# Attention and feed-forward kernel: seven buffers for the outputs of block products, sums by halves, and another order of the last pair's products

## Chip, cores and metric

One core of a Trainium2 chip. The time is device microseconds from the first to the last instruction as the host's timing of the execution sees it; the profile's own span is some 1.8 us shorter (214.0 against 215.77 for the same execution).

## The reference

```
scores = (q @ k^T) / 8, ALiBi bias, keep j if j < 8 or 0 <= i - j < 96   # batch 4, 8 heads, 768 rows, 64
x   = softmax(scores) @ v, heads side by side                            # 3072 x 512
h   = x @ w_in                                                           # 512 -> 2048
g   = s * relu(h)^2 + b
out = g @ w_out                                                          # 2048 -> 512, float32
```

## The kernel before

The rows are worked in 12 granules of 256. For each granule: scores on TensorE (PE), exponentials on ScalarE (ACT), mask on VectorE (DVE), product with v, normalization (DVE), then the first feed-forward matrix in "quarters" (`unit_p1`: 16 matmuls, two ReLUs, one square). The second matrix is applied to two granules (even `e` and odd `o`) together by a scheme of seven block products instead of eight. It needs sums of blocks of the left operand (`g_sum`, DVE), and each product is evicted into partial results or an output block that is stored.

```python
def unit_p1(j, q):
    ...                                   # 2 x (8 matmuls, ReLU on ACT)
    if j % 2:
        outs.append(lambda: nc.vector.tensor_tensor(gs, gs, gs, ALU.mult))
    else:
        nc.scalar.activation(gs, gs, ACT.Square)
...
def store(pr, row, col, ps, add):
    o = work.tile([P, GB, CH], F32, name="o_q", tag="o_sb", bufs=3)
    scaled(o[:].rearrange("p a c -> p (a c)"), ps, add)   # DVE: ps * s + add
    put(pr, row, col, o[:])                               # store on SP's queue
...
def step(s, c0, c1, c2, pool=None, pre=()):
    ...
    posts = scores(s + 1)      # PE; exponentials and masks of the next step
    run(exps); run(pre); run(masks)
    run(c0); stage_A(2 * s); flush()          # flush: evictions and squares put off
    run(c1); stage_A(2 * s + 1, pool); flush()
    run(c2) ...
    if not last and SHIFT < j + 1 < NJ:
        load_voff(j + 1, eng=nc.scalar)       # SBUF to SBUF loads, issued on ACT's queue
    flush()
...
# the last pair
run([u1(e, 2), u1(e, 3), pe(pr, 1), flush])
run([u1(o, 0), flush, g_sum(pr, 3, 0), u1(o, 1), flush, g_sum(pr, 3, 1)])
run([u1(o, 2), flush, g_sum(pr, 1, 0), g_sum(pr, 2, 0), pe(pr, 7), flush])
run([u1(o, 3), flush, g_sum(pr, 1, 1), g_sum(pr, 2, 1), pe(pr, 2), flush])
run([pe(pr, 5), flush, g_sum(pr, 4), pe(pr, 6), flush, join(pr, 1), join(pr, 2), join(pr, 0)])
run([pe(pr, 4), flush])
for tb in range(GB):                          # product 3 in halves of 128 rows
    ...
```

`pe(pr, n)` is product n of pair pr: two blocks of 128 x 256, eight matmuls each. A row of 32 matmuls in a timeline is two products.

## Time and profile before

| | before |
|---|---|
| time, first three executions | 215.04, 215.28, 216.84 us |
| span of the profiled execution | 214.0 us |
| busy: PE, DVE, ACT | 202.2, 156.6, 132.9 us |

PE is busy 95% of the span. In a timeline row the columns are start, length, engine, line, operation, output and inputs, shapes, count, and in brackets the idle time before it and what ended it. I measure PE from start to start. The best milestones are the score matmuls (`ps_s`), once a step: what lies between two of them is one step.

### The profile page before, as it was taken

Reading aid. Unit: us, or ns where it says so; the run is one execution under the profiler, and the core shown is the slowest. Engines: PE = TensorE matmul, PEld = TensorE weight load, DVE = VectorE, ACT = ScalarE, POOL = GpSimd, SP = SyncE. Lnnn points to the kernel's source line nnn. Section 1 sums busy time; section 2 is a strip of 40 time slices with the busy share of each in tenths; the row PEclk is TensorE's granted clock in tenths of the full one; section 3 lists DMA queues with packets and bytes.
Section 4 is the critical chain, followed back from the end, with each engine's and each line's share of the span. In section 5 each row is a group of like instructions: output and inputs, shape, how many; then the busy total and the mean of one; then the engine's idle time right before and its main releaser. Section 6 shows DMA issues by size and latency. Waiting matters only on the chain.

```text
span 214.0 us, 5315 instructions
## 1 busy us (share of the span) xinstructions
PE 202.2 (95%) x2181; PEld 159.8 (75%) x2189; DVE 156.6 (73%) x329; ACT 132.9 (62%) x203; POOL 68.9 (32%) x90
## 2 busy tenths in 40 slices
PE   6799999999998999999999999799999999999991
PEld 2578885557866585778788888688888889888880
DVE  3787579995989666877798874498683796726693
ACT  5765669486965558687664966554967763486300
POOL 8883335898645104507308264000000000000000
PEclk9999999999999999999999999999999999999998
DMA  6999999999999997999999979973232300330014
GB/s 171 197 178 204 207 206 174 153 152 129 117 145 132 158 158 149 142 273 208 174 150 172 141 108 192 192 106 73 51 130 72 98 5 0 98 101 0 0 52 147
DMA packets 109636, 28.43 MB, mean 133 GB/s; under 512 B 97804, under 2 KB 108108, under 8 KB 109612
## 3 DMA queue, kind: packets, MB, share of 16 engines
q0 software_dynamic: 72864, 12.85, 81.5%
q1 hardware_dynamic: 35056, 13.64, 35.9%
q10 hardware_dynamic: 1692, 1.61, 3.2%
q8 instruction: 17, 0.28, 0.6%
q14 instruction: 7, 0.06, 0.1%
HBM read 27.26 MB, written 6.29 MB: 157 GB/s over the span
## 4 chain that ended last, share of the span: by engine, by line
PE 64%; DVE 13%; DMA 8%; SPq 4%; ACT 4%; issue 3%; POOL 1%; ACTq 1%; POOLq 0%; DVEq 0%
PE ps L626 30%; PE ps L825 14%; PE ps L674 10%; DMA out_dram<-o_q 4%; PE ps_av L502 4%; DMA nat<-in_q_dram 3%; DVE gsum L789 3%; SPq L367 2%; PE ps_s L448 2%; DVE xn L473 2%; DVE pt L464 2%; DVE gT L800 2%; ACT pt L457 2%; SPq L606 2%; ACT gT L636 1%
## 5 line engine op out<-in xcount | busy, mean ns | idle before, releaser
L626 PE MATMUL ps<-xT,w_in_bf 128*128 128x256 bf16 x768 | 90.4, 273 | 1.2 <-DVE o_q L834 1.2
L636 ACT ACTIVATE gT<-ps 128x512 bf16<-128x512 f32 x96 | 56.1, 598 | 45.7 <-PE ps L626 45.3
L626 PEld LDWEIGHTS <-w_in_bf 128*128 128x128 bf16 x768 | 72.8, 98 | 10.2 <-issue 1.3
L457 ACT ACTIVATE pt<-ps_s 128x1024 bf16<-128x1024 f32 (+1 forms) x44 | 39.2, 944 | 6.3 <-PE ps_s L448 4.0
L674 PE MATMUL ps<-w_out_bf,gT 128*128 128x512 bf16 x120 | 28.7, 380 | 0.5 <-issue 0.2
L464 DVE TENSOR_TENSOR pt<-pt,tmpl 128x1024 bf16<-128x1024 bf16 (+1 forms) x40 | 24.9, 647 | 5.6 <-ACT pt L457 5.3
L825 PEld LDWEIGHTS <-gsum 128*128 128x128 bf16 x256 | 24.2, 98 | 4.6 <-DVE gsum L789 1.6
L105 POOL DMA_DIRECT2D nat<-in_k_dram x22 | 19.7, 895 | 8.2 <-DMA w_in_bf<-in_moe_w_in_dram 4.2
L106 POOL DMA_DIRECT2D vb<-in_v_dram x22 | 19.9, 906 | 7.0 <-DMA nat<-in_k_dram 2.6
L105 POOL DMA_DIRECT2D nat<-in_q_dram x22 | 19.9, 906 | 6.5 <-DMA w_out_bf<-in_moe_w_out_dram 3.4
L473 DVE TENSOR_TENSOR xn<-ps_av,rc 128x256 bf16<-128x256 f32 x48 | 20.4, 425 | 1.6
L674 PEld LDWEIGHTS <-gT 128*128 128x128 bf16 x128 | 11.7, 98 | 13.0
L825 PEld LDWEIGHTS <-gT 128*128 128x128 bf16 x192 | 18.6, 98 | 2.4
L502 PEld LDWEIGHTS <-pt 128*128 128x128 bf16 x320 | 14.1, 97 | 5.6 <-DVE xn L473 3.1
L802 ACT ACTIVATE gT<-gT 128x1024 bf16<-128x1024 bf16 x16 | 16.9, 1057 | 0.5
L639 DVE TENSOR_TENSOR gT<-gT 128x512 bf16<-128x512 bf16 x32 | 13.3, 422 | 5.2 <-ACT gT L636 4.7
L502 PE MATMUL ps_av<-vb,pt 128*128 128x65 bf16 x208 | 15.4, 194 | 1.4 <-DVE xn L473 1.2
L800 DVE TENSOR_TENSOR gT<-gT 128x1024 bf16<-128x1024 bf16 x16 | 11.0, 686 | 7.4 <-ACT gT L636 7.4
L825 PE MATMUL ps<-wsub,gsum 128*128 128x256 bf16 x128 | 14.9, 273 | 0.8 <-DVE gsum L789 0.8
L111 POOL COPY gate<-xT 1x1 bf16<-1x1 bf16 x6 | 2.6, 437 | 38.0 <-DMA xT<-xn 35.5
L825 PE MATMUL ps<-w_out_bf,gT 128*128 128x256 bf16 x128 | 14.8, 273 | 0.0
L472 DVE RECIPROCAL rc<-ps_av 128x4 f32<-128x4 f32 x48 | 8.5, 178 | 8.5 <-PE ps_av L502 6.6
(106 smaller groups left out, 215.5 us busy)
## 6 DMA issues: line engine op xcount, KB each, us to landing
out_dram<-o_q SPq DMA_DIRECT2D x15, 256.0 KB, 2.2
nat<-in_k_dram POOLq DMA_DIRECT2D x22, 128.0 KB, 7.4
nat<-in_q_dram POOLq DMA_DIRECT2D x22, 128.0 KB, 7.3
vb<-in_v_dram POOLq DMA_DIRECT2D x22, 128.0 KB, 8.1
w_in_bf<-in_moe_w_in_dram POOLq DMA_DIRECT2D x4, 512.0 KB, 11.4
w_out_bf<-in_moe_w_out_dram POOLq DMA_DIRECT2D x4, 512.0 KB, 17.9
out_dram<-o_sb SPq DMA_DIRECT2D x4, 256.0 KB, 5.1
out_dram<-o_early SPq DMA_DIRECT2D x4, 256.0 KB, 6.5
```

The source lines that it names most:

```text
L105: nc.gpsimd.dma_start(t[:, n, i, :, :], rows_of(srcs[n], b, sb))
L106: nc.gpsimd.dma_start(vbuf[b % 2][:, sb, :, 0:D], rows_of(v, b, sb))
L457: nc.scalar.activation(pt[:, :, 0:ncol], ps[:, :, 0:ncol], ACT.Exp, scale=QSCALE)
L464: nc.vector.tensor_tensor(pv, pv, m.rearrange("p h a c -> p h (a c)"), ALU.mult)
L473: nc.vector.tensor_tensor(dst, av[:, :, :, 0:D], rc[:].to_broadcast((P, 2, 2, D)), ALU.mult)
L502: nc.tensor.matmul(av[:, i, hi, 0 : D + 1], lhsT=pt[:, hi, c * P : (c + 1) * P], rhs=vv, start=(n == 0), stop=(n == len(terms) - 1),)
L626: nc.tensor.matmul(ps[:, i, :], lhsT=w_in_bf[:, kc, fc * P : (fc + 1) * P], rhs=xT[j][:, kc, :], start=(kc == 0), stop=(kc == KC - 1),)
L636: nc.scalar.activation(gs, ps[:], ACT.Relu)
L674: nc.tensor.matmul(po[:], lhsT=g_of(j)[:, fc, tb * P : (tb + 1) * P], rhs=w_out_bf[:, fc, :], start=(fc == 0), stop=(fc == FC - 1),)
L800: outs.append(lambda: nc.vector.tensor_tensor(gs, gs, gs, ALU.mult))
L802: nc.scalar.activation(gs, gs, ACT.Square)
L825: nc.tensor.matmul(ps[:, tb, :], lhsT=stat[:, fc, tb * P : (tb + 1) * P], rhs=mov[:, fc, :], start=(fc == 0), stop=(fc == NH - 1),)
```

## The change

Its intent: no DVE eviction waits for a store any more, because output blocks go round in seven buffers (three old ones and four of a tag that is otherwise used at the opening); the odd granule's first sum is done in halves, so its product can begin on the first; in the last pair products 1 and 7 fill PE while the last sums are made, and what comes last is product 2, which is added to product 1's partial result alone, with its last 128 x 256 block in two parts. Not in its title: the even granule's last quarter is squared on DVE, not on ACT.

```diff
-        if j % 2:
+        if j % 2 or q == 3:
             outs.append(lambda: nc.vector.tensor_tensor(gs, gs, gs, ALU.mult))
...
+    def out_tile():
+        n_out[0] += 1
+        tag, bufs = (("first", 4), ("o_sb", 3))[n_out[0] % 2]
+        return work.tile([P, GB, CH], F32, name="o_q", tag=tag, bufs=bufs)
     def store(pr, row, col, ps, add):
-        o = work.tile([P, GB, CH], F32, name="o_q", tag="o_sb", bufs=3)
+        o = out_tile()
... (the same in join; product 6's result gets a tile of its own in the last pair)
-            [u1(o, 3)],
-            [g_sum(pr, 1), pe(pr, 7), g_sum(pr, 2)],
+            [u1(o, 3), g_sum(pr, 1, 0)],
+            [g_sum(pr, 1, 1), pe(pr, 7), g_sum(pr, 2)],
...
-    run([u1(e, 2), u1(e, 3), pe(pr, 1), flush])
+    run([u1(e, 2), u1(e, 3), flush])
     run([u1(o, 0), flush, g_sum(pr, 3, 0), u1(o, 1), flush, g_sum(pr, 3, 1)])
-    (four lines: products 7, 2, 5, 6, 4, then 3 in two halves)
+    run([u1(o, 2), flush, g_sum(pr, 1, 0), g_sum(pr, 2, 0)])
+    run([u1(o, 3), flush, g_sum(pr, 1, 1), g_sum(pr, 2, 1), pe(pr, 1), flush, pe(pr, 7), flush])
+    run([g_sum(pr, 4), pe(pr, 5), flush, pe(pr, 6), flush, join(pr, 1), join(pr, 2), join(pr, 0)])
+    run([pe(pr, 4), flush, pe(pr, 3), flush])
+    for tb, c0, c1 in ((0, 0, CH), (1, 0, P), (1, P, CH)):
+        ...                                   # product 2
```

More of the change, by code (lines that the diff above doesn't have):

```diff
@@ L805, with product @@
     res = {}
-    def product(pr, n, tbs=range(GB), ps=None):
+    def product(pr, n, tbs=range(GB), ps=None, cols=None):
         j = 2 * pr
@@ L819, in product @@
         mov = {1: w11, 2: w21, 3: w22, 4: t4, 5: t1, 6: t2, 7: t3}[n]
+        cs = slice(0, CH) if cols is None else cols
         if ps is None:
@@ L825, in product @@
                 nc.tensor.matmul(
-                    ps[:, tb, :],
+                    ps[:, tb, cs],
                     lhsT=stat[:, fc, tb * P : (tb + 1) * P],
-                    rhs=mov[:, fc, :],
+                    rhs=mov[:, fc, cs],
                     start=(fc == 0),
@@ L844, in both_blocks, with put @@
         return ap.unsqueeze(1).to_broadcast((P, GB, CH))
-    def put(pr, row, col, o, tb=None):
+    def put(pr, row, col, o, tb=None, c0=0):
         b, g = divmod(2 * pr + row, NGR)
@@ L852, in put @@
             t0 += tb * P
-            nc.sync.dma_start(out[t0 : t0 + P, cs], o)
+            c0 += col * CH
+            nc.sync.dma_start(out[t0 : t0 + P, c0 : c0 + o.shape[-1]], o)
         else:
             nc.sync.dma_start(out[t0 : t0 + GT, cs].rearrange("(a p) c -> p a c", p=P), o)
+    n_out = [0]
+    def out_tile():
+        n_out[0] += 1
+        tag, bufs = (("first", 4), ("o_sb", 3))[n_out[0] % 2]
+        return work.tile([P, GB, CH], F32, name="o_q", tag=tag, bufs=bufs)
     def store(pr, row, col, ps, add):
-        o = work.tile([P, GB, CH], F32, name="o_q", tag="o_sb", bufs=3)
+        o = out_tile()
         scaled(o[:].rearrange("p a c -> p (a c)"), ps, add)
@@ L874, in evac @@
             ]
-        r0, r1, r7 = (t[:].rearrange("p a c -> p (a c)") for t in res[pr])
+            res[pr].append(out_tile() if pr == NJ // 2 - 1 else res[pr][0])
+        r0, r1, r7, r6 = (t[:].rearrange("p a c -> p (a c)") for t in res[pr])
         if n == 1:
@@ L882, in evac @@
         elif n == 6:
-            scaled(r0, ps, r0)
+            scaled(r6, ps, r0)
         elif n == 7:
@@ L888, in evac @@
         elif n == 4:
-            store(pr, 1, 0, ps, r0)
+            store(pr, 1, 0, ps, r6)
     def join(pr, n):
         def go():
-            r0, r1, r7 = (t[:].rearrange("p a c -> p (a c)") for t in res[pr])
+            _, r1, r7, r6 = (t[:].rearrange("p a c -> p (a c)") for t in res[pr])
             if n == 1:
-                add_f32(r1, r1, r0)
+                add_f32(r1, r1, r6)
             elif n == 0:
-                add_f32(r0, r0, r7)
+                add_f32(r6, r6, r7)
             else:
-                o = work.tile([P, GB, CH], F32, name="o_q", tag="o_sb", bufs=3)
+                o = out_tile()
                 add_f32(o[:].rearrange("p a c -> p (a c)"), r7, r1)
@@ L1170 @@
     e, o = 2 * pr, 2 * pr + 1
-    run([u1(e, 2), u1(e, 3), pe(pr, 1), flush])
+    run([u1(e, 2), u1(e, 3), flush])
     run([u1(o, 0), flush, g_sum(pr, 3, 0), u1(o, 1), flush, g_sum(pr, 3, 1)])
-    run([u1(o, 2), flush, g_sum(pr, 1, 0), g_sum(pr, 2, 0), pe(pr, 7), flush])
-    run([u1(o, 3), flush, g_sum(pr, 1, 1), g_sum(pr, 2, 1), pe(pr, 2), flush])
-    run([pe(pr, 5), flush, g_sum(pr, 4), pe(pr, 6), flush, join(pr, 1), join(pr, 2), join(pr, 0)])
-    run([pe(pr, 4), flush])
-    for tb in range(GB):
-        ps = ps_sc.tile([P, GB, 4 * P], F32, name="ps_last", tag="sc")
-        product(pr, 3, [tb], ps[:, :, 0:CH])
-        o = work.tile([P, CH], F32, name="o_last", tag="o_sb", bufs=3)
-        scaled(o[:], ps[:, tb, 0:CH], res[pr][1][:, tb, :])
-        put(pr, 0, 1, o[:], tb)
+    run([u1(o, 2), flush, g_sum(pr, 1, 0), g_sum(pr, 2, 0)])
[3 more added lines that the diff above has]
+    for tb, c0, c1 in ((0, 0, CH), (1, 0, P), (1, P, CH)):
+        if tb:
+            ps = ps_sc.tile([P, GB, 4 * P], F32, name="ps_last", tag="sc")[:, :, 0:CH]
+        else:
+            ps = ps_h.tile([P, GB, CH], F32, name="ps_2", tag="psh")[:]
+        product(pr, 2, [tb], ps, slice(c0, c1))
+        o = work.tile([P, c1 - c0], F32, name="o_last", tag="first", bufs=4)
+        scaled(o[:], ps[:, tb, c0:c1], res[pr][0][:, tb, c0:c1])
+        put(pr, 0, 0, o[:], tb, c0)
 _INS = ['q', 'k', 'v', 'n_global', 'n_local', 'moe_w_in', 'moe_w_out', 'moe_s', 'moe_b']
```

## The prediction

> **What bounds the kernel now.** I read the page's busy table and slices first, then the waits of TensorE (PE), the chain that ended last, and the timeline around each wait and at the end.
>
> The slices and the table by stage:
>
> ```profile
> PE   6799999999998999999999999799999999999991
> ...
> 160.00:180.00 20.00, 20.00 (x233) 17.36 (x231) 13.04 (x25) 13.73 (x20) 0.00 (x0) 1.00 0.20 55
> ```
>
> The reader is to see that PE is at 9 nearly throughout, and that a stage without waits shows 20.00 us busy of 20.00 at full clock. So in the second half nothing shortens the kernel but the few places where PE stands, and the end, where PE is done. VectorE (DVE) has 73% and ScalarE (ACT) 62%. The waits of PE:
>
> ```profile
> PE ps L626 <- DVE o_q L834: 1.2, 1, 1.2
> ...
> PE ps_av L502 <- DVE xn L473: 1.2, 3, 0.6
> PE ps L825 <- DVE gsum L789: 0.8, 2, 0.5
> ```
>
> The first and the third row are what the change is aimed at. The chain says where the first comes from:
>
> ```profile
> 128.29 6.75 DMA out_dram<-o_q
> 135.05 0.02 issue
> 135.07 0.76 DVE o_q L834
> 135.84 0.04 issue
> 135.88 1.92 PE ps L626 x16
> ```
>
> A store of an output block took 6.75 us to land, where the median of these stores is 2.2 us. There are three such buffers, so the DVE eviction that needs the fourth waited for it, the PSUM tile stayed taken, and PE stood. The end, in the timeline:
>
> ```profile
> 207.39 1.91 PE L825 MATMUL ps_last<-w_out_bf,gsum 128*128 128x256 bf16 x16
> 207.40 0.69 DVE L864 TENSOR_TENSOR o_q<-part,part 128x512 f32<-128x512 f32 x1
> 208.01 0.68 DVE L864 TENSOR_TENSOR part<-part,part 128x512 f32<-128x512 f32 x1
> 208.79 0.75 DVE L834 SCALAR_TENSOR_TENSOR o_q<-ps,s_bc,part 128x512 f32<-128x512 f32 x1
> 209.45 0.48 DVE L834 SCALAR_TENSOR_TENSOR o_last<-ps_last,s_bc,part 128x256 f32<-128x256 f32 x1
> 210.03 1.24 SPq L853 DMA_DIRECT2D out_dram<-o_last  x2
> 210.41 0.48 DVE L834 SCALAR_TENSOR_TENSOR o_last<-ps_last,s_bc,part 128x256 f32<-128x256 f32 x1 [0.49 <-DMA out_dram<-o_q]
> ```
>
> PE's last 16 matmuls begin at 207.39. Undisturbed blocks of 16 begin 1.75 us apart (205.64 and 207.39), so PE is free at 207.39 + 1.75 = 209.14. DVE is behind it with three additions and evictions, then waits 0.49 us for a buffer and ends at 210.89. From there to the end at 214.0 are 3.1 us of issue, landing and close.
>
> **What the Trainium skill says.** "Perfetto Trace Analysis", section on the Tensor Engine instruction: a matmul's reported end is computed, not observed. The trace agrees: 16 matmuls are shown as 1.91 us though the next 16 start after 1.75. So I size PE's losses by start to start, not by the idle column. "DMA: Bandwidth & Descriptors", section on queues, rings and completion order: each DMA engine takes turns between the queue rows that have work. Here the 6.75 us store ran while the software queue of the loads had 96.6% of the time of 16 engines from 120 to 137 us; quiet stores took 2.2. "VectorE: DVE Perf Modes", section on the TRN2 errata: an operation from SBUF pays a fixed cost per instruction, so halves cost more than a whole. Trace: a sum of 2048 elements took 1.23 us, one of 1024 took 0.69, so two halves cost 0.15 more.
>
> **The change part by part.**
>
> 1. *Seven output buffers.* The outputs alternate between the three old ones and four buffers that the opening and the early outputs used before and that are free by then. No memory or instruction is added. Before the stall the last of eight small matmuls starts at 134.47 and takes 0.03 of PE's time, so PE could have gone on at 134.50; it went on at 135.88. **1.38 us** come back. The store of the pair before may still land late; four more buffers hold that.
>
> 2. *The odd granule's first sum by halves* (three pairs). At the second of the two waits the scores (16 matmuls) start at 143.93 and the product at 145.04, so 1.11 us; undisturbed it is 152.50 to 153.05, so 0.55: 0.56 lost. At the first, 111.70 to 112.61, so 0.91: 0.36 lost. The third (176.95) has none. The order of DVE's instructions in the new kernel puts the first half ahead of a normalization, the second half behind the last square. DVE is busy all through (109.47 to 112.56), so the sum isn't finished earlier: two times 0.69 for 1.23, 0.15 later. But the product's first four matmuls (4 x 0.11 = 0.44 us) need only the first half, so they can start, and 0.44 of each wait is covered less the 0.15. I take 0.29 of 0.36 and 0.41 of 0.56 (in the second, the second half ends some 0.6 after PE comes free, and 0.15 stay): **0.70 us**.
>
> 3. *The even granule's last quarter is squared on DVE* (in the diff, not in the title; four times): ACT loses 4 x 1.06 us, DVE gains 4 x 0.69. Neither is the bound. In the first pair ACT's queue goes from the square at 97.36 to two DMA issues at 97.44 and 98.96, and the exponentials wait behind these until 99.86. Without the square the issues can start behind the activation at 96.73, 0.63 earlier. Then the masks at 100.91 and the normalization at 102.65 come earlier by as much, and the wait of PE behind them (100.86 to 103.13 for 16 matmuls and eight small ones, 2.27 instead of 1.75) loses its 0.52. Against it, DVE can square only when it has done the template copies at 98.8, so to about 99.45; the second product reaches that quarter at 98.93 + 0.44 = 99.37: about 0.15 new wait. Net **0.37 us**.
>
> 4. *The last pair's order.* Products 1 and 7 go behind the last granule's four quarters. Before, products 7 and 5 each waited for a half of a sum: 16 matmuls took 196.65 to 198.52 (1.87) and 32 took 202.02 to 205.64 (3.62), 0.12 lost in each. After it, 3.5 us of ready products lie between the last quarter and product 5: **0.24 us**.
>
> 5. *The end.* Let PE be free at E. Products 4, 3 and 2 (1.75 us each) now follow product 6, so product 6 ends at E - 5.25. DVE after a product starts some 0.26 after the next block's first matmul (205.64 and 205.90). So: eviction of 6 at E - 5.0 (0.75), three additions (0.69 each) to E - 2.2, eviction of 4 to E - 1.4, of 3 from E - 1.4 to E - 0.65, the first block of product 2 (0.48) to E - 0.15, then its two parts of 128 columns. Their cost is an estimate from 0.75 for 512 elements and 0.48 for 256: 0.35 each. The last waits for the matmuls: E + 0.26 to E + 0.6. Before it was 210.89 - 209.14 = 1.75 behind E: **1.15 us**. The 16 added matmuls of 128 columns take the place of eight of 256, the same columns, so PE pays nothing or 0.1. The last store has 64 KB instead of 128 KB; landings were 1.7 and 2.1: **0.15 us** less.
>
> Sum: 1.38 + 0.70 + 0.37 + 0.24 + 1.15 + 0.15 = 4.0 us. I hold back 0.3 us for matmul blocks of 128 columns and for waits that move instead of going: **3.7 us**, so 215.28 - 3.7 = 211.6 us.
>
> **The rivals.**
>
> *A new wait takes the place of the one removed.* Once PE runs 1.4 us earlier from 134.5, transposes by DMA or ACT could be late. For it: the chain before 128.29 runs through the SP queue, which is full of transposes, and the outputs are queued behind them. Against it: the transposes from 139 to 145 serve a granule that is read more than 5 us later, and ACT's waits for PE (45.3 us in all) say it has room. It would leave 1.5 to 2.5 us of gain: 213 us.
>
> *DVE becomes the bound between the sums and at the end.* For it: it is full from 109.47 to 112.56 and in the last 7 us; it gets 4 squares and three half sums. If the normalization that now stands behind a half sum held up PE (the next small matmuls use a single PSUM buffer), parts 2 and 3 would give nothing: gain 2.9, 212.4 us. Against it: that normalization is 2 us ahead of its reader.
>
> *The end is hidden anyway.* If the six last stores queue on SP (0.37 to 0.5 us an issue) and the DMA, the last landing would not follow the last eviction. For it: stores come every 0.4 us. Against it: 256 KB quiet move inside their 2.2 us, and the SP issues keep up. It would take 0.7 off: 212.3 us.
>
> *All is had, and more*: part 1 also frees DVE, and no wait comes: 4.3 us, 211.0 us.
>
> **Range and chances.** All parts point one way, none adds work to PE, so slower needs an unforeseen stall. Two rivals together give 213; the best case 210.8. Range 210.7 to 213.0. Faster by over 2% needs below 210.97, which the full sum of 4.0 just misses: 0.2. Within 2%: 0.78. Slower: 0.02.
>
> **What would show it.** In the profile after: no wait of PE for DVE at the output block, and no wait of DVE for a DMA of an output; PE's waits for the sums below 0.3 us together, the remaining one in four matmuls' distance after the product's start; the exponentials of the first pair about 0.6 us earlier relative to their scores, the 0.35 us wait at the small matmuls gone, and perhaps a small new wait of PE for the square on DVE; in the last pair no wait of PE for a sum; the last eviction ending 0.5 to 0.8 us after PE is free, and 2.8 to 3.1 us from there to the end. The prediction is wrong if PE's idle time comes back at another place, above all at scores that wait for a transpose, or if the tail from PE's last matmul to the end stays above 4.5 us.

## More of the kernel before

Semaphore times (when a DMA's landing was counted) are not in the views of the profile; they are read from the kept trace files.

Buffers of one tag go round; the build decides which of the three PSUM buffers a tile gets.

## The result, and the profile after

| | before | changed |
|---|---|---|
| median | 215.54 us (215.04 to 216.84, 4 runs) | 213.44 us (213.28 to 213.68, 4 runs) |
| ratio | | 0.9894 (0.9848 to 0.9940) |
| span of the profiled execution | 214.0 | 211.9 |

A ratio is the mean time of one kernel's fast runs over that of the other's of the same rounds, so not quite the ratio of the medians; the interval is 95%. In later rounds the changed kernel had 213.64 and the ratio 0.9882 (0.9846 to 0.9918). So it is faster by 2.1 to 2.5 us. I had predicted 3.7, and a range that ends at 213.0: the direction was right, the size wrong. Some of the miss in the absolute time is the base: I reckoned from 215.28, and the kernel before had 215.54 here and 215.88 in the later rounds.

The waits of PE in the changed kernel's first trace (engine, line, what ended the wait: us in total, times, longest):

```profile
PE ps_av L502 <- DVE xn L473: 1.7, 3, 0.9
...
PE ps L626 <- DVE o_q L835: 0.3, 1, 0.3
```

The wait of PE for the sums (0.8 us before) is off the list, as predicted. The wait for the output block, 1.2 us at 135.88 before, is gone from its place; the 0.3 us on the list is a new one, elsewhere. And the wait at the small matmuls, which I had expected to shrink, has grown from 1.2 to 1.7 (in the second traces below it is 1.6 before and 1.4 after, so this list alone shows no loss). The end, in the timeline:

```profile
207.22 1.06 PE L826 MATMUL ps_last<-w_out_bf,gT 128*128 128x128 bf16 x16
207.42 0.48 DVE L835 SCALAR_TENSOR_TENSOR o_last<-ps,s_bc,part 128x256 f32<-128x256 f32 x1
207.87 0.80 DVE L835 SCALAR_TENSOR_TENSOR o_last<-ps_last,s_bc,part 128x128 f32<-128x128 f32 x2
207.93 1.41 SPq L855 DMA_DIRECT2D out_dram<-o_last  x3
```

PE is free at 207.22 + 0.87 = 208.09, and DVE ends at 208.67, 0.58 behind it where it was 1.75. From there to the end are 3.23 us (before 3.11).

Where the unforeseen loss is, the timeline of PE in the first pair shows. Before:

```profile
96.63 0.62 PE L448 MATMUL ps_s<-qx,kx 64*128 64x128 bf16 x16
97.18 3.67 PE L825 MATMUL ps<-w_out_bf,gT 128*128 128x256 bf16 x32
100.68 0.34 PE L502 MATMUL ps_av<-vb,pt 128*128 128x65 bf16 x6
100.86 1.91 PE L626 MATMUL ps<-xT,w_in_bf 128*128 128x256 bf16 x16
103.13 0.35 PE L502 MATMUL ps_av<-vb,pt 128*128 128x65 bf16 x6 [0.35 <-DVE xn L473]
103.32 1.91 PE L626 MATMUL ps<-xT,w_in_bf 128*128 128x256 bf16 x16
105.16 0.62 PE L448 MATMUL ps_s<-qx,kx 64*128 64x128 bf16 x16
```

And in the changed kernel:

```profile
96.74 0.62 PE L448 MATMUL ps_s<-qx,kx 64*128 64x128 bf16 x16
97.29 3.78 PE L826 MATMUL ps<-w_out_bf,gT 128*128 128x256 bf16 x32
100.91 0.34 PE L502 MATMUL ps_av<-vb,pt 128*128 128x65 bf16 x6
101.09 1.91 PE L626 MATMUL ps<-xT,w_in_bf 128*128 128x256 bf16 x16
103.89 0.35 PE L502 MATMUL ps_av<-vb,pt 128*128 128x65 bf16 x6 [0.89 <-DVE xn L473]
104.54 1.91 PE L626 MATMUL ps<-xT,w_in_bf 128*128 128x256 bf16 x16 [0.30 <-DVE o_q L835]
106.38 0.62 PE L448 MATMUL ps_s<-qx,kx 64*128 64x128 bf16 x16
```

From scores to scores it was 105.16 - 96.63 = 8.53 us and is 106.38 - 96.74 = 9.64: 1.11 us lost, where I had expected 0.37 gained. Three things are new: the 32 matmuls take 3.62 from start to start of what follows instead of 3.50; the small matmuls come 2.80 behind the quarter instead of 2.27; and the next quarter waits for the eviction of the output block.

### The profile page after: what moved, and what is told of

It is laid out like the page before. It is cut to its first block, busy times and chain, and to the rows that moved or that the text cites. A ratio compares the mean times of both kernels' runs of the same rounds, so it can differ in the third digit from the quotient of the medians.

```text
span 211.9 us, 5336 instructions
## 1 busy us (share of the span) xinstructions
PE 202.3 (95%) x2189; PEld 159.8 (75%) x2197; DVE 159.9 (75%) x337; ACT 128.5 (61%) x199; POOL 67.8 (32%) x90
## 4 chain that ended last, share of the span: by engine, by line
PE 79%; DMA 8%; DVE 6%; issue 2%; ACT 1%; POOL 1%; SPq 0%; POOLq 0%; ACTq 0%; DVEq 0%
PE ps L626 35%; PE ps L826 21%; PE ps L674 10%; PE ps_av L502 4%; PE ps_s L448 4%; DMA xT<-xn 3%; DMA nat<-in_q_dram 3%; DVE pt L464 1%; DVE xn L473 1%; DMA vo<-vb 1%; ACT pt L457 1%; DVE o_early L707 1%; PE ps_t L358 1%; PE ps_s L524 1%; PE ps_s L539 1%
## 5 line engine op out<-in xcount | busy, mean ns | idle before, releaser
L800 DVE TENSOR_TENSOR gT<-gT 128x1024 bf16<-128x1024 bf16 x20 | 13.7, 685 | 11.9 <-ACT gT L636 11.9
L826 PE MATMUL ps<-w_out_bf,gsum 128*128 128x256 bf16 x128 | 15.3, 273 | 0.0
L826 PE MATMUL ps<-w_out_bf,gT 128*128 128x256 bf16 x120 | 14.1, 273 | 0.0
L111 POOL COPY gate<-xT 1x1 bf16<-1x1 bf16 x6 | 1.5, 258 | 38.7 <-DMA xT<-xn 36.2
```

What stands on the lines that cost most here:

```text
L826: nc.tensor.matmul(ps[:, tb, cs], lhsT=stat[:, fc, tb * P : (tb + 1) * P], rhs=mov[:, fc, cs], start=(fc == 0), stop=(fc == NH - 1),)
```

## The experiments

Names with `a_` start from the changed kernel, with `b_` from the kernel before.

**Theory S:** the square on DVE causes the loss in the first pair. **Rival L:** it is chance, the landing of a DMA. **Theory M**, formed after the first four runs: the stall at the output block in the kernel before ends when a store lands; what is lost ahead of it hides in it, so the stall is worth less than one trace shows. Against it: a fixed stall.

### after_again: the changed kernel unedited, a second trace

> The changed kernel once more, unedited, for a second trace. In the first trace the stretch from the scores at 96.74 to the scores at 106.38 took 9.64 us on TensorE, against 8.53 in the kernel before (96.63 to 105.16); that 1.11 us is what I had not foreseen. Theory S (the square on DVE in the first pair causes it): the stretch is again 9.4 to 9.8 us and the time 213.4. Rival L (the landing of the activation transposes, 98.07 instead of about 97.4, is chance from run to run): the stretch differs by over 0.4 us from the first trace.

213.64 us, ratio 0.9882. The stretch took 106.59 - 97.70 = **8.89** us, not 9.64. So both have a part: 0.36 more than before stays, and 0.75 comes and goes. ACT in this stretch, first trace:

```profile
96.22 1.23 ACT L636 ACTIVATE gT<-ps 128x512 bf16<-128x512 f32 x2
98.17 1.44 ACTq L315 DMA_DIRECT2D vo<-vb  x1
99.71 0.81 ACTq L316 DMA_DIRECT2D vo<-vb  x1
100.62 1.94 ACT L457 ACTIVATE pt<-ps_s 128x1024 bf16<-128x1024 f32 x2 [3.18 <-DMA vo<-vb]
```

Second trace:

```profile
97.17 1.23 ACT L636 ACTIVATE gT<-ps 128x512 bf16<-128x512 f32 x2
98.36 1.42 ACTq L315 DMA_DIRECT2D vo<-vb  x1
99.88 0.85 ACTq L316 DMA_DIRECT2D vo<-vb  x1
100.83 1.94 ACT L457 ACTIVATE pt<-ps_s 128x1024 bf16<-128x1024 f32 x2 [2.43 <-DVE gT L800]
```

The reader is to compare the first DMA issue with the end of the two ReLUs ahead of it: 98.36 against 97.17 + 1.23 = 98.40 in the second trace, but 98.17 against 97.45 in the first. There the chain that ended last has, for the 0.7 us between:

```profile
90.66 7.41 DMA xT<-xn
...
98.17 2.45 DMA vo<-vb
```

The built program shows why one waits for the other: eight semaphores serve the DMAs of the SP and ACT queues in turn, and this issue has the semaphore of that transpose, so it waits for it to land. In the first trace that was at 98.07, 0.62 behind the ReLUs.

The semaphore times of all traces show that this is no exception. With the square on DVE the issue starts 0.10 us after this landing in each of six traces: the landing is at 98.07, 98.25, 97.93, 97.27, 98.23 and 98.81 (first and second trace of the changed kernel, b_sq_first, a_dup4, a_whole_sum, a_half), and the exponentials start 2.5 to 2.6 us after it. That the issue of the second trace falls together with the end of the ReLUs is chance; in a_dup4 it starts at 97.37, before they end (97.64). With the square on ACT the landing came 0.5 to 0.9 us before the issue in four traces (96.97 against 97.44 in the first of the kernel before), so there the square's start set the issue; in b_dup4 it came 0.10 us before it. The 0.75 us between the two traces of the changed kernel are this landing: 1.33 us after the start of the scores in one, 0.55 in the other.

### a_sq_late: the first pair's last quarter squared on ACT again

```diff
-        if j % 2 or q == 3:
+        if j % 2 or (q == 3 and j > 4):
```

> The changed kernel, but in the first pair the even granule's last quarter is squared on ACT as before. Theory S: the stretch of the first pair falls from 9.64 to about 8.5 us, as in the kernel before, and the time by 1.1 us to about 212.3. The build gives the first tile of the quarter after product 2 the PSUM buffer that it had before the change, so the wait for the output's eviction goes too. Rival L: no change beyond chance, 213.4, and the exponentials still start over 3.5 us after the scores.

The stretch took 105.74 - 97.20 = **8.54**, as in the kernel before (8.53), and no wait for an output block is on the list. In time, 213.54 us and 0.9879: not different from the changed kernel. 0.35 us is within what six runs tell (213.02 to 214.15), so the trace, not the time, carries this.

### b_sq_first: this square alone in the kernel before

```diff
-        if j % 2:
+        if j % 2 or (q == 3 and j == 4):
```

> The kernel before with nothing of the change but this one square on DVE (first pair only). Theory S: slower than before by about 1.1 us (216.4 where before has 215.3), the stretch of the first pair 9.4 to 9.8 us. Rival L: same as before within 0.3 us. If the loss is only the exchanged PSUM buffer and the wait for the square, it is 0.5 us.

The stretch took 106.28 - 97.39 = **8.89**, the same 0.36 more, by the same two waits:

```profile
97.94 3.78 PE L825 MATMUL ps<-w_out_bf,gT 128*128 128x256 bf16 x32
101.56 0.35 PE L502 MATMUL ps_av<-vb,pt 128*128 128x65 bf16 x6
101.74 1.91 PE L626 MATMUL ps<-xT,w_in_bf 128*128 128x256 bf16 x16
103.79 0.36 PE L502 MATMUL ps_av<-vb,pt 128*128 128x65 bf16 x6
104.44 1.80 PE L626 MATMUL ps<-xT,w_in_bf 128*128 128x256 bf16 x15 [0.30 <-DVE o_q L834]
```

Start to start: 3.62 for 3.50 (product 2 waits for the square, 0.12, as predicted); 2.05 for 2.27 (the exponentials come 0.1 earlier, 0.22 gained); and 0.65 for 0.19 (0.46 lost to the output's eviction). The last is not a matter of data. With the square on DVE the build gives the next quarter's first tile the PSUM buffer of product 2, which is free only after its eviction; before, it gave it one that a ReLU had freed. The two built programs show the two buffers exchanged. The time ratio is 1.0014 (0.9967 to 1.0062), 0.3 us slower; but this interval reaches from 0.7 us faster to 1.3 slower and holds Theory S's 1.1 us too, so here as well the trace decides.

0.36 is what one pair of traces shows. Over all traces with the loads ahead of the exponentials the stretch took 8.53 to 8.80 us with this square on ACT (five traces) and 8.82 to 9.04, once 9.64, with it on DVE (six): about 0.3 us.

### a_vo: the loads behind the exponentials

```diff
-            load_voff(j + 1, eng=nc.scalar)
+            late_vo.append(j + 1)       # issued in the next step, right after run(exps)
```

> The changed kernel with the loads of the shifted values issued on ACT's queue behind the next step's exponentials instead of ahead of them. If what makes the exponentials late in the first pair is that ACT's queue stands at that DMA issue, which waits for an earlier DMA to land, then they start less than 1.5 us after the scores, the normalization is in time, the stretch falls from 9.64 to 8.0 to 8.3 us, and the time by about 1.4 us to 212.0, although the square stays on DVE and the PSUM buffers stay exchanged. If the square or the buffer alone is what costs, it stays at 9 us or more.

The stretch took 105.11 - 96.98 = **8.13**, though the square stays on DVE and the buffers stay exchanged, and the exponentials start 0.60 us after the scores (97.58 against 96.98), where they started 3.23 after them before (99.86 against 96.63):

```profile
97.58 1.02 ACT L457 ACTIVATE pt<-ps_s 128x1024 bf16<-128x1024 f32 x1
98.18 1.42 ACTq L315 DMA_DIRECT2D vo<-vb  x1
```

212.67 us, ratio 0.9851 (0.9811 to 0.9891). So the wait at the small matmuls came from ACT's queue standing at two DMA issues, the first of which waits for a landing (here at 98.08, when the exponentials had begun). In time less was won than the 1.4 that I had written, which counted the varying part in full: by the two ratios of the same rounds 0.7 us, by the medians 1.0.

### before_again: the kernel before unedited, a second trace

> The kernel before, unedited, for a second trace. Theory M (the stall at the output block ends when a store lands, and what TensorE loses ahead of it is hidden in it): the scores of the first pair come later or earlier than 96.63 by some tenths, the wait at the output block is shorter by about as much as they are later, and the scores behind it (137.72 in the first trace) move less than half as far. Rival: the stall is a fixed 1.2 us and everything behind it moves along.

```profile
136.41 1.91 PE L626 MATMUL ps<-xT,w_in_bf 128*128 128x256 bf16 x16 [0.64 <-DVE o_q L834]
138.25 0.51 PE L448 MATMUL ps_s<-qx,kx 64*128 64x128 bf16 x12
```

(A single run; its clock was 0.994.) PE came 1.11 us later than in the first trace (scores at 129.43 for 128.32), and the scores behind the stall only 0.53 later (138.25 for 137.72): the step took 8.82 us, not 9.40, and the stall was 0.80, not 1.38. In the 14 traces the scores of the first pair come between 96.63 and 98.28 us; the trace from which I had sized the stall has the earliest.

### b_bufs: the seven buffers alone

```diff
-        o = work.tile([P, GB, CH], F32, name="o_q", tag="o_sb", bufs=3)
+        o = out_tile()                  # seven buffers, as in the change
```

> The kernel before with the seven output buffers alone. The wait at the output block goes (1.38 us start to start). If it is a fixed 1.38, the time falls by 1.4 us (ratio 0.9935). Theory M: in most executions TensorE arrives there later than in the first trace by some tenths, so the gain is 0.6 to 1.2 us (ratio 0.995 to 0.997); in the trace the stretch of that step is 8.0 us instead of 9.4.

The step took 137.45 - 129.43 = 8.02: the stall is gone. The time is 215.15 us, ratio **0.9969** (0.9945 to 0.9994), so 0.7 us faster. Theory M gave 0.995 to 0.997; a fixed 1.38 us (0.9935) lies just outside the interval. That says that 1.38 was too much; it doesn't tell Theory M from a stall that is simply shorter in most executions.

### b_dup4 and a_dup4: eight matmuls twice, ahead of the stall's place

```diff
-            product(pr, n)
+            product(pr, n, (0, 1, 1) if (pr, n) == (2, 4) else range(GB))
```

> The kernel before, with eight matmuls of the first pair's product 4 done twice (0.87 us more on TensorE, the result the same), after the store that will be waited for has had its data and ahead of the wait for it. Theory M: the wait shrinks by about 0.87 us, to 0.3 to 0.5 us, and the time stays (ratio 1.000 to 1.001). Rival, a fixed stall: 0.87 us slower (1.004).

> The changed kernel with the same eight matmuls twice. There is no wait behind them to hide them, so both theories say 0.87 us slower than the changed kernel (213.64 and 213.44 so far): 214.4, a ratio to before of 0.992 instead of 0.988. If it costs clearly less, something else takes up delays in the changed kernel.

In the kernel before, the scores ahead of the stall came at 130.28, 0.85 later than in its second trace, and those behind it at 138.30, 0.05 later:

```profile
136.46 1.91 PE L626 MATMUL ps<-xT,w_in_bf 128*128 128x256 bf16 x16
138.30 0.51 PE L448 MATMUL ps_s<-qx,kx 64*128 64x128 bf16 x12
```

The wait is gone, which looks as if all 0.87 us had been hidden in it. The semaphore times say otherwise for this trace. Its store was issued at 128.85 and landed at 134.32, 5.5 us later; in the second trace it landed at 135.58. The eviction that needs the buffer began at 135.23; without the added matmuls it would have begun near 134.38 (an estimate, 135.23 - 0.85; b_bufs has it at 134.38), with the buffer already free. So this execution had no wait to hide them in, and what made up for them was an early landing.

The times leave it open too. In the kernel before the ratio is 1.0021 (0.9996 to 1.0047), which holds Theory M's 1.000 to 1.001 and the fixed stall's 1.004. In the changed kernel it is 0.9932, where it had 0.9882 unedited in other rounds: about 1 us by the ratios, 0.5 by the medians (214.15 and 213.64), and 0.87 in the trace (the step took 9.00 for 8.13). So it is not shown that the stall hides work put just ahead of it.

### b_vo: the loads behind the exponentials, in the kernel before

The edit of a_vo.

> The kernel before with the loads of the shifted values issued behind the exponentials, nothing else. The first pair's stretch falls from 8.53 to about 8.0 us as in the changed kernel with this edit (8.13). Theory M (the stall at the output block swallows what is gained or lost ahead of it): the wait there grows by 0.3 to 0.5 us, and the time stays within 0.3 us of before (ratio 0.998 to 1.001). Rival, a fixed stall: 0.5 us faster or more (0.9975 or less).

The stretch fell to 105.30 - 97.29 = 8.01 as expected, and the wait at the output block was 0.9 us, longer than in the second trace (0.6) and shorter than in the first (1.2). But the time was 214.85 us, ratio 0.9955 (0.9931 to 0.9979): 1.0 us faster, where Theory M allowed 0.3. As I had put it, M fails here. The scores behind the stall came at 137.49, earlier than in both traces of the kernel before. What fits the four traces with the stall (these three and b_sq_first): the transposes ahead of that store on SP's queue start with PE (at 119.34, 120.46 and here 119.48), the store is issued behind them (128.29, 128.97 and 127.76) and lands 6.6 to 7.1 us later. So what PE wins or loses before that moves the transposes too: from the first trace to the second PE came 1.11 us later and the landing 0.53 (135.05 and 135.58). The stall was 1.38 and 1.01 us where PE was early (scores at 120.19 and 120.33) and 0.80 and 0.81 where it was late (121.30 and 121.31). But the landing also varies by itself, down to 5.5 us after the issue in b_dup4. In the four traces the last of the store's sixteen completion signals came 1.0 to 1.9 us after the fifteenth, in b_dup4 0.4: the eviction waits for the slowest part. This reading was made after the runs; how much of a delay the stall hides is not tested by itself.

### a_whole_sum: the first sum in one piece again

```diff
-            [u1(o, 3), g_sum(pr, 1, 0)],
-            [g_sum(pr, 1, 1), pe(pr, 7), g_sum(pr, 2)],
+            [u1(o, 3)],
+            [g_sum(pr, 1), pe(pr, 7), g_sum(pr, 2)],
```

> The changed kernel with the odd granule's first sum in one piece again. The halves are worth what the traces show, 0.25 us in the first pair (8.49 to 8.24 from scores to scores) and 0.37 in the second (8.57 to 8.20): those two stretches go back to 8.5 and 8.6, and the time rises by 0.6 us (ratio 0.991 where the changed kernel has 0.988). Rival: the sum's wait is hidden by another and the stretches stay: no change.

```profile
PE ps L826 <- DVE gsum L789: 0.8, 2, 0.5
```

The waits are back, the two stretches took 121.54 - 113.05 = 8.49 and 152.47 - 143.89 = 8.58, as expected. The ratio is 0.9932 (0.9903 to 0.9961), against 0.9902 of a_half in the same rounds: 0.6 us, as expected, though the intervals overlap. The median of its six runs is 214.33; one of them, 216.6, was slow and is not in the ratio.

### a_half: the last block in one piece

```diff
-    for tb, c0, c1 in ((0, 0, CH), (1, 0, P), (1, P, CH)):
+    for tb, c0, c1 in ((0, 0, CH), (1, 0, CH)):
```

> The changed kernel with its last block of 128 x 256 in one piece, not in two parts of 128 columns. My prediction had the last eviction 0.13 us later (0.48 for 0.35) and the last landing of 128 KB 0.15 later. If a landing doesn't depend on these sizes (1.7 to 2.1 us for 128 KB before, 1.9 to 2.2 after), and SP has one issue less to make, only 0.0 to 0.1 us is lost or nothing at all: ratio 0.988 to 0.989.

Last eviction:

```profile
209.02 0.48 DVE L835 SCALAR_TENSOR_TENSOR o_last<-ps_last,s_bc,part 128x256 f32<-128x256 f32 x1 [0.39 <-PE ps_last L826]
```

PE is free at 208.81 (207.94 + 0.87), DVE ends 0.69 later, the span 3.10 after that: 3.79 in all, against 3.81 with the split. 213.51 us, 0.9902 (0.9878 to 0.9926). The two parts bring nothing: the last eviction ends 0.11 us earlier, but the issue of its store starts only 0.27 after it (208.94), behind the two issues ahead of it on SP's queue, where in one piece it starts 0.03 after it. The landing itself took about as long, 1.65 us for 64 KB and 1.71 for 128 KB by the semaphore times.

### a_best: what the runs pointed to, together

a_vo, the square of the first pair on ACT, and the last store but one issued on ACT's queue.

> The changed kernel with three edits: the loads of the shifted values behind the exponentials; the first pair's last quarter squared on ACT again; and the last store but one issued on ACT's queue, so that the very last doesn't wait for its issue on SP. Stretch of the first pair 8.0 us, where the changed kernel has 8.9 to 9.6; from the end of the last eviction to the end 3.0 us instead of 3.2. Time 212.3 to 212.6 us, ratio 0.983 to 0.985; the run with the first edit alone had 0.9851.

The stretch took 105.69 - 97.69 = 8.00, and from the last eviction (207.98) to the end (211.1) 3.1 us. 212.76 us, ratio 0.9861 (0.9835 to 0.9888), a little short of what I expected. It ran in other rounds than a_vo (212.67, 0.9851) and can't be told from it, so of the three edits only the loads behind the exponentials is seen to help. Both beat the kernel before and, by 0.5 to 0.7 us by the ratios, the changed one (0.9882), which ran in a_vo's rounds; the intervals overlap.

## Why the prediction was wrong

The sum that I had put together failed in step 3, whose sign was wrong (0.72 us), in the size of step 1 (0.58) and, less, of step 5 (0.26). The second traces of both kernels are a fair pair: the scores of the first pair come at 97.74 and 97.70. From milestone to milestone the changed kernel's difference to the kernel before is:

| step of the prediction | predicted, us | second traces, us |
|---|---|---|
| 1 seven buffers (scores to scores, 8.82 to 8.02) | 1.38 | 0.80 |
| 2 sum by halves (8.49 to 8.24 and 8.57 to 8.21) | 0.70 | 0.61 |
| 3 square on DVE (8.54 to 8.89) | 0.37 | -0.35 |
| 4 the last pair's order (last scores to PE free: 40.39 to 40.12) | 0.24 | 0.27 |
| 5 the end (PE free to end: 4.82 to 3.78) | 1.30 | 1.04 |
| sum | 4.0 | 2.4 |

The spans differ by the same 2.4 us (214.5 and 212.1), and the two timed ratios of the change give 2.3 and 2.5.

**Step 1** had the right mechanism: the stall goes completely. Its size was wrong, because "it went on at 135.88" was taken from one trace as a constant. It is a wait for a landing: 1.38, 0.80, 0.81 and 1.01 us in the four traces that have it, none in that of b_dup4, where the store landed early, and 0.7 us in the time of b_bufs. The trace that I sized it from has the longest. Whether a part of it hid other delays is argued, not shown. The rival that I had written, that waits move rather than go, was about what comes after; I had not asked how long the wait is in other executions.

**Step 2** was right within 0.1: halves start the product and don't finish the sum sooner. a_whole_sum confirms it. The prediction's own rule (0.44 less 0.15) gives 0.29 for each of the two waits; it took 0.41 for the second, and 0.36 was measured.

**Step 3** failed, and with its sign. "Without the square the issues can start behind the activation at 96.73, 0.63 earlier" looked at the order on ACT's queue and not at what the first issue itself waits for. That is the landing of the transpose whose semaphore it shares. In the trace that I read it came at 96.97, ahead of the square's start at 97.36, and didn't show; without the square it ends the wait in all six traces, 0.3 to 1.3 us after the scores begin. So the exponentials started 2.9 to 3.9 us after their scores, where they had started 3.23 after them and my gain needed 2.6; in b_sq_first taking the square away brought 0.1. What I had weighed as 0.15 of new wait for the square was 0.12 there (0.69 in the trace of a_dup4, which has no wait for the output block in this stretch). What I had not looked for at all is that the build then exchanged two PSUM buffers, which cost 0.46: I compared the order of instructions and not the buffers behind the names.

**Step 4** was right in size; no run of its own isolates it. **Step 5** was right as to DVE (0.58 behind PE, predicted 0.6). Its last term, 0.15 for a smaller last store, was wrong: the last store landed 1.65 us after its issue where it had been 1.72, but its issue came 0.27 after the eviction where it had been 0.03, and a_half shows no gain.

The rivals: waits did take the place of those removed, at the PSUM buffer and at an issue that waits for a transpose to land, and not at scores; DVE did not become the bound between the sums; the last landing follows the last eviction, but for the 0.27 us at SP's queue. What stays open is why PE comes to the first pair between 96.63 and 98.28 in traces of kernels that don't differ up to there, and what sets the landing of that transpose, which in the 14 traces came between 0.1 us before and 1.3 us after the start of these scores.

## What to carry to other kernels

A wait for a DMA has no fixed length: before counting it as a gain, take a second trace, and read in each when the landing came. That a wait is gone from a trace with more work ahead of it doesn't show yet that the work was hidden: the landing may have been early. When instructions move, compare which buffer each tile gets and which landing each DMA issue waits for, not only the order. DMA issues on a computing engine's queue stand ahead of its work: issue them behind what others wait for.

## What the Trainium skill lacked or had wrong

- "DMA: Bandwidth & Descriptors", section on the anatomy of one DMA: its fit of a fixed 2.0 us and a part that grows with size gives 2.6 us for 256 KB (an estimate by the page's figures, which are for DMAs issued from GpSimd); the quiet stores, issued from SP, took 2.2. In the last stores the size hardly showed: 1.65 and 1.9 us for 64 KB, 1.7 to 2.2 for 128 KB. I found no figure for how far a store is delayed when the software queue of loads is busy; here it landed 6.6 to 7.1 us after its issue in four traces and 5.5 in another.
- "Perfetto Trace Analysis": I found no duration in it for what two DMA issues on ACT's queue cost the activation behind them: 1.42 to 1.58 and 0.78 to 0.85 us of issue, and exponentials that start 2.9 to 3.9 us after their scores instead of 0.6 (a_vo) or, with the square ahead of them, 1.7 (b_vo and a_best).
- None of the pages that I read says that DMAs of two queues which share a semaphore in turn wait for each other's landing; here one issue on ACT's queue started 0.10 us after the landing of a transpose of SP's queue in eight traces, and in one of them had stood 0.7 us for it.
